# The last V unit dealt to the DMA engines in three parts, W2's remainder in two, and four casts into two result rows

## The chip, the cores and the metric

The kernel runs on one core of a Trainium2 chip. The metric is the device time of one execution in microseconds (us); lower is better. TensorE is PE in the profile (its weight loads are PEld), VectorE is DVE, ScalarE is ACT, GpSimd is POOL, and SyncE, which issues nearly all transfers, is SP. All transfers are carried out by 16 DMA engines.

## The reference

Two tokens pass through one attention block that decodes against a cache, and through one feed-forward block; a gate mixes the results. All tensors are bf16.

```python
B, Sq, D = 2, 1, 512
Hq, Hkv, Sk, Dh = 32, 32, 4096, 128      # k_cache and v_cache: (2, 32, 4096, 128), 64 MB each
Dff = 1376

g = sigmoid((x * gate_w).sum(-1, keepdims=True))
q = (x @ wq)                                             # per head
p = softmax(q @ k_cache^T * Dh ** -0.5)
a = (p @ v_cache).reshape(B, Sq, Hq * Dh) @ wo           # wo: (4096, 512)
b = relu(x @ w1) @ w2                                    # w1: (512, 1376), w2: (1376, 512)
out = g * a + (1 - g) * b                                # (2, 1, 512)
```

## The kernel before

**The caches.** K and V are each read in 16 units of 16384 rows. A unit is a `[128, 16384]` bf16 tile of `kv`: each of 128 partitions gets 128 consecutive cache rows, 32 KB in one piece. `kv` has three slots (`NSLOT`). The list `order` says in which order units are loaded: four K units, then K and V units in turn, then the last four V units (12 to 15). `place` is a unit's number in that list; slot and semaphore follow from it. SP issues unit n as soon as unit n-3 has been used up (`freed`). A transfer adds 16 to its slot's semaphore when it has landed, and `slot_wait` says which value a reader waits for.

**The work on a unit.** A K unit is transposed in four turns by DVE (`k_turn`, L381) and multiplied with the queries on PE (`k_scores`, L397) into a bank of PSUM; after every four units `sm_max`, `sm_exp` and `sm_spread` make the softmax numerators, which POOL copies to `ptm`. A V unit is multiplied on PE with them in 32 matmuls (`v_unit`, L443) and then added up from four masked pieces on DVE (`v_extract`, L454 and L457). After eight V units `o_gather` (L473 to L484) divides by the denominators, applies the gate and turns the result of one token into `oW`: 128 partitions, 32 row groups, one column for each token. The order of the work is written out by hand in one loop over 64 K turns, and a loop over V units 12 to 15 after it.

**The ends.** The result is `oW` times wo plus `hT` (the gated ReLU of x @ w1, `ffn_relu`) times w2. It is added up in one PSUM bank at column `FIN_C0`: `fin_row` (L489) multiplies one row group with four blocks of 128 columns, and block c goes to a partition group of its own, at partitions 32c onwards. `project` runs 32 row groups of wo (128 matmuls of 128 columns), `ffn_f` the 11 row groups of w2 (44 matmuls; row group 10, which has 96 rows, first). `oW` and `hT` are 32 columns wide: token 0 is column 0, token 1 is column 16, the rest is zeros from memsets on POOL (L242, L243), and `fin_row` takes 17 columns as lhsT. So the two tokens of block c come out at partitions 32c and 32c+16, with zeros between. A memset on DVE (L494) clears the bank before, one DVE cast (L508) brings all 128 partitions to `out_sb`, and the store (L276) takes every 16th partition of it, eight pieces of 256 B.

**SP's queue after the last unit.** The wo tile lies where wq and w1 were (`wreg`). In order: the last V unit (L266), eleven transfers of w2's last 96 rows (`W2A`, L271; rows 0-13, 14-26 and so on, 1 KB a row), wo in two halves (`wo0`, `wo1`, L272 and L273, 16 KB a partition each), w2's other rows in three parts (`w2b`, `w2c`, `w2d`, L275: 4, 4 and 2 KB a partition), the store. `project` waits for `wo0` at row group 0 and for `wo1` at row group 16; `ffn_f` for `w2a` at group 10, and for the other parts at groups 0, 4 and 8.

Of the kernel before, what the change touches and what calls it, by code (L numbers as in the profile page):

```python
# [3 lines left out]
dt = mybir.dt  # L4
ALU = mybir.AluOpType
ACT = mybir.ActivationFunctionType
# [6 lines left out]

NSLOT = 3
NKT = 3
W2A = ((0, 14), (14, 27), (27, 39), (39, 50), (50, 60), (60, 69), (69, 77), (77, 84), (84, 90), (90, 94), (94, 96))


class _Marker:
# [67 lines left out]
def bass_gated_mix__gqa_block_cached__dense_activation_relu__decode_kernel(  # L87
# [18 lines left out]
    sb = nc.alloc_sbuf_tensor  # L106
# [11 lines left out]
    kv = sb("kv", [128, NSLOT, 16384], dt.bfloat16)  # L118
    xTw = sb("xTw", [128, 4, 32], dt.bfloat16)
    qrow = sb("qrow", [128, 2, 4, 128], dt.bfloat16)  # L120
    wreg = sb("wreg", [128, 16384], dt.bfloat16)
    w2 = sb("w2", [128, 11, 512], dt.bfloat16)
# [18 lines left out]
    s4 = sb("s4", [32, 4, 128], dt.bfloat16)  # L141
    X2 = sb("X2", [128, 2, 8, 128], dt.float32)
    O_sb = sb("O_sb", [32, 2, 128], dt.bfloat16)
    oW = sb("oW", [128, 32, 32], dt.bfloat16)
    hT = sb("hT", [128, 11, 32], dt.bfloat16)
    out_sb = sb("out_sb", [128, 128], dt.bfloat16)

    PSF = nc.alloc_psum_tensor("PS", [128, 4096], dt.float32)
    PSB = PSF[:, :].bitcast(dt.bfloat16)
# [3 lines left out]
    def psf(p0, p1, c0, n):  # L153
        return PSF[p0:p1, c0:c0 + n]
# [8 lines left out]
    H_C0 = MISC + 72  # L163
    L_C0 = MISC + 96
    O_C0 = MISC + 128
    R_C0 = MISC + 256
    FIN_C0 = 0
# [4 lines left out]
    sem = {n: nc.alloc_semaphore("sem_" + n) for n in names}  # L172
    sem_slot = [nc.alloc_semaphore(f"sem_slot{s}") for s in range(NSLOT)]
# [3 lines left out]
    def marker(name):  # L177
        m = mk.get(name)
        if m is None:
            m = _Marker()  # L180
            mk[name] = m
        return m


    order = [("k", u) for u in range(4)]
# [3 lines left out]
    place = {what: n for n, what in enumerate(order)}  # L189

    def slot_of(what):
        return place[what] % NSLOT

    def slot_wait(what):
        return (sem_slot[slot_of(what)], 16 * (place[what] // NSLOT + 1))

    def freed(what):
        kind, u = what
# [3 lines left out]
    def pool(fn, waits=(), signal=None):  # L202
        P.add("pool", fn, waits=[marker(w) for w in waits], signal=marker(signal) if signal else None)

    def dve(fn, waits=(), signal=None, dwaits=()):
        P.add("dve", fn, waits=[marker(w) for w in waits], signal=marker(signal) if signal else None, dwaits=dwaits)

    def act(fn, waits=(), signal=None, dwaits=()):
        P.add("act", fn, waits=[marker(w) for w in waits], signal=marker(signal) if signal else None, dwaits=dwaits)

    def pe(fn, waits=(), signal=None, dwaits=()):
        P.add("pe", fn, waits=[marker(w) for w in waits], signal=marker(signal) if signal else None, dwaits=dwaits)
# [5 lines left out]
         waits=["c_i16z"], signal="c_i16")  # L218
# [8 lines left out]
         waits=["c_m3z"], signal="c_m3")  # L227
# [4 lines left out]
         waits=["c_s1"], signal="c_s2")  # L232
# [6 lines left out]
         waits=["c_s4z"], signal="c_s4")  # L239
    pool(lambda g: g.memset(selx[:], 0.0), signal="c_selx")  # L240
    pool(lambda g: g.memset(ptm[:], 0.0), signal="c_ptm")
    pool(lambda g: g.memset(hT[:], 0.0), signal="c_hT")  # L242
    pool(lambda g: g.memset(oW[:], 0.0), signal="c_oW")  # L243


    wq_in = A_wq.rearrange("(p t) n -> p (t n)", t=4)
# [6 lines left out]
    def unit_in(what):  # L253
        kind, u = what
        rows = k_rows if kind == "k" else v_rows
        return rows[u * 16384:(u + 1) * 16384, :].rearrange("(p r) d -> p (r d)", p=128)

    def sp(fn, waits=(), dwaits=()):
        P.add("sp", fn, waits=waits, dwaits=dwaits)
# [3 lines left out]
    sp(lambda e: e.dma_start(wreg[:, :], wq_in).then_inc(sem["wq"], 16))  # L263
    for n, what in enumerate(order):
        waits = [freed(order[n - NSLOT])] if n >= NSLOT else []
        sp(lambda e, what=what: e.dma_start(kv[:, slot_of(what), :], unit_in(what)).then_inc(sem_slot[slot_of(what)], 16),  # L266
           waits=waits)
        if n == 2:
            sp(lambda e: e.dma_start(wreg[:, 0:5504], w1_in).then_inc(sem["w1"], 16), waits=[marker("pe_q")])
    for p0, p1 in W2A:  # L270
# [2 lines left out]
    sp(lambda e: e.dma_start(wreg[:, 8192:16384], wo_in[:, 8192:16384]).then_inc(sem["wo1"], 16))  # L273
    for name, r0, r1 in (("w2b", 0, 4), ("w2c", 4, 8), ("w2d", 8, 10)):
        sp(lambda e, name=name, r0=r0, r1=r1: e.dma_start(w2[:, r0:r1, :], w2a_in[:, r0:r1, :]).then_inc(sem[name], 16))  # L275
    sp(lambda e: e.dma_start(out.rearrange("b s (c n) -> c (b s) n", n=128),  # L276
                             out_sb[0::16, :]).then_inc(sem["out"], 16),
       waits=[marker("dve_out")])
    sp(lambda e: e.wait_ge(sem["out"], 16))


# [83 lines left out]

    def ffn_relu():
        for b in range(2):
            dve(lambda v, b=b: v.tensor_scalar(out=hT[:, 0:10, 16 * b], in0=PSF[:, H_C0 + b:H_C0 + 20:2], scalar1=0.0,
                                               scalar2=gm[:, b:b + 1], op0=ALU.max, op1=ALU.mult),
                waits=["pe_h", "dve_gm", "c_hT"])  # L370
            dve(lambda v, b=b: v.tensor_scalar(out=hT[0:96, 10, 16 * b:16 * b + 1], in0=psf(0, 96, H_C0 + 20 + b, 1), scalar1=0.0,
                                               scalar2=gm[0:96, b:b + 1], op0=ALU.max, op1=ALU.mult),
                waits=["pe_h", "dve_gm"], signal=f"dve_h{b}")

# [47 lines left out]
    def sm_spread(g):  # L422
        dve(lambda v: v.transpose(out=ET_sb[:, :], in_=E_sb[:, :]),  # L423
            waits=[f"act_exp{g}"] + ([f"pool_pt{g - 1}_3"] if g else []), signal=f"dve_et{g}")
        for hq in range(4):
            pool(lambda e, g=g, hq=hq: e.tensor_copy(  # L426
                out=ptm[32 * hq:32 * hq + 32, g % 2, :, :, :, hq, :],
                in_=ET_sb[32 * hq:32 * hq + 32, :].rearrange("p (r u a c) -> p r u a c", r=16, u=4, a=2)),
                waits=[f"dve_et{g}", "c_oW"] + ([f"pe_v_{4 * g - 5}"] if g >= 2 else []), signal=f"pool_pt{g}_{hq}")


    def v_unit(v):
# [38 lines left out]
    def o_gather(b):  # L471
        for u in range(8):
            pe(lambda e, u=u, b=b: e.matmul(psf(0, 32, O_C0, 128), lhsT=selx[:, 28 - 4 * u:60 - 4 * u], rhs=X2[:, b, u, :],  # L473
                                            start=(u == 0), stop=(u == 7)),
               waits=[f"dve_x{8 * b + u}_3"] + ([f"dve_rinv{b}", "dve_selx"] if u == 0 else []),
               signal=(f"pe_O{b}" if u == 7 else None))
        dve(lambda v, b=b: v.tensor_scalar(out=O_sb[:, b, :], in0=psf(0, 32, O_C0, 128), scalar1=rinv[:, b:b + 1],
                                           scalar2=gb[0:32, b:b + 1], op0=ALU.mult, op1=ALU.mult),
            waits=[f"pe_O{b}", f"dve_rinv{b}", "dve_g"], signal=f"dve_O{b}")
        for dq in range(4):  # L480
            pe(lambda e, dq=dq, b=b: e.matmul(psf(0, 128, R_C0 + 32 * b, 32), lhsT=s4[:, dq, :], rhs=O_sb[:, b, 32 * dq:32 * dq + 32],
                                              start=(dq == 0), stop=(dq == 3), tile_position=(0, 0)),
               waits=([f"dve_O{b}", "c_s4"] if dq == 0 else []), signal=(f"pe_R{b}" if dq == 3 else None))
        dve(lambda v, b=b: v.tensor_copy(out=oW[:, :, 16 * b], in_=psf(0, 128, R_C0 + 32 * b, 32)), waits=[f"pe_R{b}", "c_oW"], signal=f"dve_oW{b}")  # L484


    def fin_row(r, first, last, lhsT, rhs, dw, waits, signal):
        for c in range(4):
            pe(lambda e, c=c: e.matmul(psf(32 * c, 32 * c + 17, FIN_C0, 128), lhsT=lhsT, rhs=rhs[:, c * 128:(c + 1) * 128],  # L489
                                       start=first, stop=last, tile_position=(0, 32 * c), skip_group_check=True),  # L490
               dwaits=(dw if c == 0 else []), waits=(waits if c == 0 else []), signal=(signal if c == 3 else None))

    def project():
        dve(lambda v: v.memset(psf(0, 128, FIN_C0, 128), 0.0), waits=["act_exp2"], signal="dve_fin0")  # L494
        for r in range(32):
            dw = {0: [(sem["wo0"], 16)], 16: [(sem["wo1"], 16)]}.get(r, [])
            fin_row(r, r == 0, False, oW[:, r, 0:17], wreg[:, r * 512:(r + 1) * 512], dw,
                    ["dve_oW0", "dve_oW1", "act_exp3", "dve_fin0"] if r == 0 else [], None)

    def ffn_f():  # L500
        for n, r in enumerate([10, *range(10)]):
            m = 96 if r == 10 else 128
            dw = {10: [(sem["w2a"], 16 * len(W2A))], 0: [(sem["w2b"], 16)], 4: [(sem["w2c"], 16)], 8: [(sem["w2d"], 16)]}.get(r, [])
            fin_row(r, False, r == 9, hT[0:m, r, 0:17], w2[0:m, r, :], dw, ["dve_h0", "dve_h1"] if n == 0 else [],
                    "pe_fin" if r == 9 else None)

    def store():
        dve(lambda v: v.tensor_copy(out=out_sb[:, :], in_=psf(0, 128, FIN_C0, 128)), waits=["pe_fin"], signal="dve_out")  # L508


    gate()
# [74 lines left out]
```

## Time and profile before

| | us |
|---|---|
| median of three runs (lowest, highest) | 347.75 (347.29, 347.83) |
| the profiled execution | 347.82 |
| its span, first to last instruction | 346.6 |
| PE busy, DVE busy | 201.8, 183.6 |
| ACT busy, POOL busy | 13.9, 22.1 |
| DMA: bytes read, mean rate over the span | 145.43 MB, 420 GB/s |
| mean granted TensorE clock | 0.818 |

The profile is of one execution. Its busy times and its timeline are counted from the start of the span; the execution's own time is 1.2 us longer than the span. Beside each engine's instructions the trace has every DMA packet with its start, duration and size, though not which DMA engine moved it. In an answer on waits, a line gives who waited, for whom, and then the time in total, how often, and the longest; in the timeline, a line gives start, duration, engine, line of the kernel, operation, output and input, and in brackets the idle time before it with what ended it.

### The profile page before, as it was taken

What the parts mean: (1) busy time and instruction counts of PE and PEld (TensorE: products, weight loads), DVE (VectorE), ACT (ScalarE), POOL (GpSimd) and SP (SyncE); (2) the same over time, 40 slices, a digit from 0 to 9 for tenths busy, and PEclk for the clock granted to TensorE, in tenths of its full rate; (3) what the DMA queues carried; (4) which work ended last, traced back from release to release, by engine and by line L of the source; (5) the groups of instructions that cost most, each with busy time, mean ns of one, the idle gap of its engine ahead of it and who ended that gap; (6) DMA issues with size and microseconds to landing.
All of it is one profiled execution on the core that took longest, in us unless ns stands there. A gap on an engine that the chain in (4) does not pass through costs nothing.

```text
span 346.6 us, 3023 instructions
## 1 busy us (share of the span) xinstructions
PE 201.8 (58%) x1318; PEld 77.5 (22%) x1334; DVE 183.6 (53%) x177; ACT 13.9 (4%) x48; POOL 22.1 (6%) x38
## 2 busy tenths in 40 slices
PE   0339969773845739174845739174885639422283
PEld 0213344221211213021211213021421213110052
DVE  0858777991908355391908365391648267211120
ACT  1040000000000000000000000000000000000000
POOL 8500000020000000020000000020000000200000
PEclk9999978999685958789695969589698969666578
DMA  8999999999999999999999999999999999999993
GB/s 314 446 446 427 402 447 435 444 427 424 424 425 428 442 439 431 429 427 427 427 433 435 439 431 425 427 431 427 435 441 431 427 431 427 419 435 442 393 409 151
DMA packets 5838, 145.61 MB, mean 420 GB/s; under 512 B 735, under 2 KB 834, under 8 KB 1218
## 3 DMA queue, kind: packets, MB, share of 16 engines
q1 hardware_dynamic: 5820, 145.43, 98.1%
q8 instruction: 10, 0.16, 0.2%
q14 instruction: 2, 0.02, 0.0%
q10 hardware_dynamic: 6, 0.00, 0.0%
HBM read 145.43 MB, written 0.00 MB: 420 GB/s over the span
## 4 chain that ended last, share of the span: by engine, by line
DMA 71%; DVE 16%; PE 10%; SPq 2%; issue 1%; DVEq 0%
DMA kv<-in_A_k_cache_dram 53%; DVE kt L381 12%; DMA w<-in_B_w_dram 10%; DMA kv<-in_A_v_cache_dram 8%; PE PS L397 6%; PE PS L443 4%; DVE X L457 1%; SPq L271 1%; DVE mpad L407 1%; DVE ET L423 1%; PE PS L489 0%; DVE X L454 0%; SPq L266 0%; DVE mrow L409 0%; DVE mmax L410 0%
## 5 line engine op out<-in xcount | busy, mean ns | idle before, releaser
L397 PE MATMUL PS<-kt,qbuf 128*128 128x512 bf16 x496 | 146.6, 447 | 95.1 <-DVE kt L381 92.2
L381 DVE STREAM_TRANSPOSE kt<-kv 128x2048 f32<-128x2048 f32 x64 | 144.0, 2285 | 101.5 <-DMA kv<-in_A_k_cache_dram 98.8
L397 PEld LDWEIGHTS PS<-kt,qbuf 128*128 128x128 bf16 x512 | 50.6, 108 | 189.1 <-DVE kt L381 116.5
L443 PE MATMUL PS<-kv,ptm 128*16 128x512 bf16 x512 | 37.2, 442 | 23.0 <-DMA kv<-in_A_v_cache_dram 23.0
L426 POOL COPY ptm<-ET 32x512 bf16<-32x512 bf16 x16 | 9.7, 607 | 275.1 <-DVE ET L423 274.4
L443 PEld LDWEIGHTS PS<-kv,ptm 128*16 128x16 bf16 x512 | 12.8, 98 | 45.8 <-issue 35.8
L454 DVE TENSOR_SCALAR X<-PS,maskc 128x128 f32<-128x128 f32 x16 | 5.1, 319 | 30.9 <-PE PS L443 30.9
L457 DVE SCALAR_TENSOR_TENSOR X<-PS,maskc,X 128x128 f32<-128x128 f32 x48 | 16.8, 351 | 1.7
L352 ACT ACTIVATE qbuf<-PS 32x4 bf16<-32x4 bf16 x32 | 5.7, 178 | 109.2 <-PE PS L397 108.6
L418 ACT ACTIVATE E<-PS,negm 128x512 bf16<-128x512 f32 x4 | 2.7, 687 | 154.5 <-DVE negm L414 154.5
L473 PE MATMUL PS<-X,selx 128*32 128x128 f32 x32 | 5.5, 346 | 0.0
L289 DVE COPY xTw<-xT 128x8 bf16<-128x8 bf16 x1 | 5.1, 5054 | 0.0
L489 PE MATMUL PS<-wreg,oW 128*17 128x128 bf16 x128 | 2.8, 257 | 3.8 <-DMA wreg<-in_A_wo_dram 3.2
L473 PEld LDWEIGHTS PS<-X,selx 128*32 128x32 f32 x32 | 4.6, 147 | 1.9 <-issue 1.4
L284 PE MATMUL PS<-ident,x_sb 3*128 3x3 bf16 x4 | 0.3, 166 | 8.2 <-POOL s L236 8.2
L290 DVE TENSOR_TENSOR xg<-xT 128x8 f32<-128x8 bf16 x1 | 4.9, 4858 | 0.0
L362 PE MATMUL PS<-xT,wreg 128*128 128x2 bf16 (+1 forms) x44 | 2.8, 200 | 3.2 <-DMA wreg<-in_B_w_dram 3.2
L287 DVE COPY xT<-PS 128x12 bf16<-128x12 bf16 x1 | 0.2, 170 | 8.5 <-PE PS L284 8.5
L508 DVE CAST out_sb<-PS 128x128 bf16<-128x128 f32 x1 | 0.3, 291 | 7.9 <-PE PS L489 7.9
L220 POOL MEMSET qbuf<- 128x5120 bf16 x1 | 4.4, 4370 | 0.0
L294 PE MATMUL PS<-xgs,ones 128*128 128x2 f32 x2 | 0.6, 364 | 5.6 <-DVE xgs L292 5.6
L407 DVE TENSOR_REDUCE mpad<-PS 128x1 f32<-128x512 f32 x4 | 2.7, 676 | 2.1 <-PE PS L397 2.1
(60 smaller groups left out, 45.2 us busy)
## 6 DMA issues: line engine op xcount, KB each, us to landing
kv<-in_A_k_cache_dram SPq DMA_DIRECT2D x16, 4096.0 KB, 26.2
kv<-in_A_v_cache_dram SPq DMA_DIRECT2D x16, 4096.0 KB, 18.7
wreg<-in_A_wq_dram SPq DMA_DIRECT2D x1, 4096.0 KB, 12.3
wreg<-in_A_wo_dram SPq DMA_DIRECT2D x2, 2048.0 KB, 30.4
wreg<-in_B_w_dram SPq DMA_DIRECT2D x1, 1376.0 KB, 25.4
w<-in_B_w_dram SPq DMA_DIRECT2D x2, 512.0 KB, 33.8
w<-in_B_w_dram SPq DMA_DIRECT2D x1, 256.0 KB, 34.4
x_sb<-in_A_x_dram ACTq DMA_DIRECT2D x1, 2.0 KB
```

Source lines behind the costliest of these rows:

```text
L220: pool(lambda g: g.memset(qbuf[:], 0.0), signal="c_qbuf")
L289: dve(lambda v: v.tensor_copy(out=xTw[:, :, 0:2], in_=xT), waits=["dve_xT", "c_xTw"], signal="dve_xTw")
L290: dve(lambda v: v.tensor_tensor(out=xg[:], in0=xT, in1=xT3[:, :, 2:3].to_broadcast([128, 4, 2]), op=ALU.mult), waits=["dve_xT"], signal="d ...
L352: act(lambda a, out=out, src=src: a.activation(out=out, in_=src, func=ACT.Copy), waits=[f"pe_sc_{4 * uh + 3}"], signal=f"q_1_{uh}_{hq}")
L381: dve(lambda v: v.transpose(out=dst, in_=pairs[:, :, 32 * k:32 * k + 32, :]), waits=([f"pe_sc_{i - NKT}"] if i >= NKT else []), dwaits=([s ...
L397: pe(lambda e, j=j, pos=pos, c=c, cc=cc: e.matmul(psf(0, 128, (g % 2) * BANK, 512), lhsT=qbuf[:, u % 8, j, 32 - pos:160 - pos], rhs=kt16[: ...
L407: dve(lambda v, g=g: v.tensor_reduce(out=mpad[:, 0:1], in_=psf(0, 128, (g % 2) * BANK, 512), axis=AX.X, op=ALU.max), waits=[f"pe_sc_{16 * ...
L426: pool(lambda e, g=g, hq=hq: e.tensor_copy(out=ptm[32 * hq:32 * hq + 32, g % 2, :, :, :, hq, :], in_=ET_sb[32 * hq:32 * hq + 32, :].rearra ...
L443: pe(lambda e, n=n, t=t, a=a, r16=r16, grp=grp, u4=u4, rows=rows: e.matmul(psf(32 * t, 32 * t + 16, V_B * BANK, 512), lhsT=ptm[:, grp % 2, ...
L454: dve(lambda e, src=src, dst=dst: e.tensor_scalar(out=dst, in0=src, scalar1=maskc[:, 0:1], scalar2=None, op0=ALU.mult), waits=[f"pe_v_{v}" ...
L457: dve(lambda e, src=src, dst=dst, c=c: e.scalar_tensor_tensor(out=dst, in0=src, scalar=maskc[:, c:c + 1], in1=dst, op0=ALU.mult, op1=ALU.add),
L473: pe(lambda e, u=u, b=b: e.matmul(psf(0, 32, O_C0, 128), lhsT=selx[:, 28 - 4 * u:60 - 4 * u], rhs=X2[:, b, u, :], start=(u == 0), stop=(u ...
```

## The change

The last V unit is issued as three transfers into the same slot, under the same semaphore: partitions 0 to 111, 112 to 124 and 125 to 127 (112 rows over all DMA engines, 13 over engines 0 to 12, 3 over engines 0 to 2). `slot_wait` counts the three. W2's last 96 rows are issued as 91 and 5 rows, no longer in eleven pieces. `oW` and `hT` are two columns wide, their memsets and that of the PSUM bank are gone, and a matmul of `fin_row` writes two partitions. Four casts, two on DVE and then two on ACT, bring the four blocks to two rows of `out_sb`, and the store writes two rows of 1 KB.

```diff
-W2A = ((0, 14), (14, 27), (27, 39), (39, 50), (50, 60), (60, 69), (69, 77), (77, 84), (84, 90), (90, 94), (94, 96))
+W2A = ((0, 91), (91, 96))
+DEAL = ((0, 112), (112, 125), (125, 128))
...
-    oW = sb("oW", [128, 32, 32], dt.bfloat16)
-    hT = sb("hT", [128, 11, 32], dt.bfloat16)
-    out_sb = sb("out_sb", [128, 128], dt.bfloat16)
+    oW = sb("oW", [128, 32, 2], dt.bfloat16)
+    hT = sb("hT", [128, 11, 2], dt.bfloat16)
+    out_sb = sb("out_sb", [2, 512], dt.bfloat16)
...
+    def pieces(what):
+        return DEAL if what == order[-1] else ((0, 128),)
+
     def slot_wait(what):
-        return (sem_slot[slot_of(what)], 16 * (place[what] // NSLOT + 1))
+        return (sem_slot[slot_of(what)], 16 * (place[what] // NSLOT + len(pieces(what))))
...
-    pool(lambda g: g.memset(hT[:], 0.0), signal="c_hT")
-    pool(lambda g: g.memset(oW[:], 0.0), signal="c_oW")
...
-        sp(lambda e, what=what: e.dma_start(kv[:, slot_of(what), :], unit_in(what)).then_inc(sem_slot[slot_of(what)], 16),
-           waits=waits)
+        for p0, p1 in pieces(what):
+            sp(lambda e, what=what, p0=p0, p1=p1: e.dma_start(kv[p0:p1, slot_of(what), :], unit_in(what)[p0:p1, :])
+               .then_inc(sem_slot[slot_of(what)], 16), waits=(waits if p0 == 0 else []))
...
-    sp(lambda e: e.dma_start(out.rearrange("b s (c n) -> c (b s) n", n=128),
-                             out_sb[0::16, :]).then_inc(sem["out"], 16),
-       waits=[marker("dve_out")])
+    sp(lambda e: e.dma_start(out.rearrange("b s n -> (b s) n"), out_sb[:, :]).then_inc(sem["out"], 16),
+       waits=[marker("dve_out"), marker("act_out")])
...
-            pe(lambda e, c=c: e.matmul(psf(32 * c, 32 * c + 17, FIN_C0, 128), lhsT=lhsT, rhs=rhs[:, c * 128:(c + 1) * 128],
+            pe(lambda e, c=c: e.matmul(psf(32 * c, 32 * c + 2, FIN_C0, 128), lhsT=lhsT, rhs=rhs[:, c * 128:(c + 1) * 128],
...
-        dve(lambda v: v.memset(psf(0, 128, FIN_C0, 128), 0.0), waits=["act_exp2"], signal="dve_fin0")
...
-        dve(lambda v: v.tensor_copy(out=out_sb[:, :], in_=psf(0, 128, FIN_C0, 128)), waits=["pe_fin"], signal="dve_out")
+        def piece(c):
+            return out_sb[:, 128 * c:128 * c + 128], psf(32 * c, 32 * c + 2, FIN_C0, 128)
+
+        for c in range(2):
+            dst, src = piece(c)
+            dve(lambda v, dst=dst, src=src: v.tensor_copy(out=dst, in_=src), waits=["pe_fin"], signal=("dve_out" if c else None))
+        for c in range(2, 4):
+            dst, src = piece(c)
+            act(lambda a, dst=dst, src=src: a.activation(out=dst, in_=src, func=ACT.Copy), waits=["pe_fin"],
+                signal=("act_out" if c == 3 else None))
```

## The prediction

> **What bounds the kernel now.** First the page's slices:
>
> ```profile
> DMA  8999999999999999999999999999999999999993
> ```
>
> The 16 DMA engines are busy from the first slice to the last but one, while no compute engine is. So the end is set by the bytes, and by how evenly the engines finish. Next the busy time by stage, in the windows of the tail (columns: window, length, busy time and instructions of PE, PEld, DVE, ACT, POOL, the granted clock, the DMA share, GB/s):
>
> ```profile
> 325.00:329.20 4.20, 0.04 (x4) 0.07 (x8) 0.00 (x0) 0.00 (x0) 0.00 (x0) 0.50 1.01 371
> 336.60:341.00 4.40, 1.12 (x68) 0.94 (x72) 0.00 (x0) 0.00 (x0) 0.00 (x0) 1.00 0.89 363
> 341.00:344.50 3.50, 3.23 (x108) 2.40 (x108) 0.00 (x0) 0.00 (x0) 0.00 (x0) 0.52 0.15 57
> ```
>
> Until 336 us DMA is full; from 341 us a few late engines carry 57 GB/s. The waits of the tail say who waits for them:
>
> ```profile
> PE PS L443 <- DMA kv<-in_A_v_cache_dram: 6.4, 1, 6.4
> PE PS L489 <- DMA wreg<-in_A_wo_dram: 3.2, 1, 3.2
> PE PS L489 <- DMA w<-in_B_w_dram: 0.2, 1, 0.2
> ```
>
> PE waits for the last V unit, for the second half of wo and for the w2 parts, each a transfer that every engine has a share of. The timeline shows the end word for word:
>
> ```profile
> 329.16 3.59 PE L443 MATMUL PS<-kv,ptm 128*16 128x512 bf16 x32 [6.37 <-DMA kv<-in_A_v_cache_dram]
> 336.43 0.17 DVE L494 MEMSET PS<- 128x128 f32 x1
> 336.65 1.07 PE L489 MATMUL PS<-wreg,oW 128*17 128x128 bf16 x64 [0.58 <-DVE PS L494]
> 340.95 1.75 PE L489 MATMUL PS<-wreg,oW 128*17 128x128 bf16 x64 [3.23 <-DMA wreg<-in_A_wo_dram]
> 343.43 1.03 PE L489 MATMUL PS<-w,hT 128*17 128x128 bf16 x24 [0.20 <-DMA w<-in_B_w_dram]
> 344.52 0.29 DVE L508 CAST out_sb<-PS 128x128 bf16<-128x128 f32 x1 [7.92 <-PE PS L489]
> 344.84 0.65 SPq L276 DMA_DIRECT2D out_dram<-out_sb  x1
> ```
>
> Last, the trace's DMA packets (start, duration, bytes; no engine's name). A packet starts 3 to 4 ns before the one ahead of it on its engine ends, so they can be chained into 16 rows of packets. Each has 264 of 32 KB; the numbers of 1 KB packets are 11, 11, 10, 10, 9, 9, 8, 7, 6, 5, 4, 3, 2, 1, 0, 0, as eleven W2A pieces of n rows on engines 0 to n-1 give. I number the chains by that (two with the same count can't be told apart). Four things are read there:
> - A 32 KB packet has a mean of 1.218 us on every chain, so no engine is slower than another.
> - What sets engines apart is single stops: a 16 KB packet of the instruction queue sits about 1.0 us on one engine, which loses about 1.5 us by it. Nine fall between 41.7 and 333.7 us, the last on engine 6.
> - Engines without a stop end the last V unit at 326.5 to 327.2 us, those with one at 328.3 to 328.9.
> - Behind the V unit, a chain's time to the end of wo's first half, less eight 16 KB packets (8 x 0.608 = 4.87), is 1.0 to 1.45 us on engines 0 to 7, 0.58 on 8, 0.35 on 9 and 0.1 to 0.3 on 10 to 15. So many tiny packets cost more than their own 46 ns each: the three wo packets after them are slowed by about 0.3 us each.
>
> Engine 6 ends last, at 343.9 us, then 2 or 3 (342.8) and 5 (342.4); the rest between 339.9 and 342.0.
>
> **The change, part by part.** The profiled run took 347.82 us (span 346.6 and 1.2 around it); the median is 347.75. I count from 347.82.
>
> *W2A in two transfers.* Engines 0 to 12 get seven 1 KB rows under one completion, 0 to 4 one more with another. That is 8 to 10 packets instead of engine 6's 16; the nearest row is engine 9 (10 packets, 0.35 us). Engine 6 loses 1.10 us now by the same working, stop taken out, so it gains 0.75 us, and wo's second half, w2b, w2c and w2d come that much earlier together. Bounds: nothing (the excess is not the number of packets) and 1.0.
>
> *SP's queue.* Five issues stand for the last unit and W2A where twelve did; W2A's eleven took 4.0 us (the chain's SPq L271), 0.36 each, so SP is done some 2.5 us earlier. At 303 us, when they are issued, the engines still have two units ahead of them, so nothing comes of it. The new slot count asks for all three parts; the unit's V matmuls still start at the last landing. Only the first of the three waits for the buffer.
>
> *The rows dealt 112, 13, 3.* Engines 0 to 2 move nine rows, 3 to 12 eight, 13 to 15 seven. By packets alone engine 2 gains a row (1.22) and loses 0.93 of W2A's excess: 342.82 + 0.29 = 343.1 us, level with engine 6 at 343.9 - 0.75 = 343.15. The lightened 13 to 15 (339.9 to 342.0) weren't last, so nothing is won there.
>
> What the trace doesn't show is a large transfer narrower than 128 partitions. In every large one, eight rows per engine follow each other at 1.218 us (26.9 GB/s), and whether the engine sets this, or the entry into the partitions that it serves, can't be read. Here thirteen neighbouring partitions are written at once by 13 engines, then three more. Lower bound: the engine sets it, 1.22 us for a row, nothing extra. Upper bound: the entry does, eight partitions to one as eight rows go to one engine; then partitions 112 to 127 have two entries, 8 x 1.22 = 9.74 us where 1.22 was counted, 8.5 extra. The 112 rows, seven a piece, then no longer match engines and entries one to one: up to one row, 1.2, more. No end is near: the only narrow transfers, W2A's, aren't free (up to 1.45 us for 96 KB), which speaks against the lower one, and sixteen partitions with only two entries would need the worst layout. I take the middle by ratio: the square root of 8 rows on one entry, 2.83 x 1.218 = 3.44 us, so 2.2 extra, and half of 1.2 for the 112 rows: 2.8 together.
>
> The Trainium skill has a rule here (SBUF — State Buffer, Door 1: The DMA port swizzle): partitions reach memory by 16 ports of about 27 GB/s, and 112 to 127 lie on four of them, so that few neighbours are slow however many engines write. By it, as an estimate from that page, sixteen rows take four rows' time, 4.9 us, 3.65 extra, and the whole sum would be about 352 us. No run here shows it.
>
> Is it hidden? Not by compute: wo and w2 stand behind these rows on the same engines, so each late row moves the end. The V path has more room: the unit would land near 332.7 (engine 2: 328.65 + 1.22 + 2.8), wo's first 64 matmuls would start 7.3 us later as now, at 340.0, and end at 341.1, before wo's second half at 340.95 + 2.0.
>
> *Memsets.* L494's 0.17 us goes, and up to 0.2 us of wait at 336.65; wo's second half is 3.2 us away, so nothing. hT's and oW's on POOL (0.38 and 0.94 us at 12.4 us) delayed nobody. lhsT of 2 columns instead of 17: the matmuls still move 128 columns each at a granted clock of 0.52; between 0 and 0.1, I take nothing.
>
> *Casts and store.* Two casts on DVE for one: a cast of 128x32 took 0.297 us and of 128x128 0.291, so the length isn't what they cost; two in a row are 0.6, that is 0.31 more. ACT's two start with them; 178 ns at 4 columns and 687 at 512 put 128 columns at 0.30, so they end together. The store's issue was 0.65 us with eight pieces; W2A's two-row issue took 0.25, so up to 0.40 less. Together -0.09 (bounds -0.3 and +0.4).
>
> Sum: -0.75 + 2.8 - 0.09 = +1.96, so 349.8 us.
>
> **The rivals.**
> 1. *Each engine keeps its pace* (other side). No extra for narrow rows: 347.82 - 0.75 - 0.09 = 347.0, faster. For it: all 16 chains run at one pace whatever else goes on. It decides if the narrow rows cost below 0.15 us.
> 2. *The gains fall out and the rows cost nothing*: W2A's excess stays on engines 2 and 6, engine 2 gets a ninth row (342.82 + 1.22 = 344.04, 0.14 later than now), the two casts cost 0.31 and the issue stays: 348.3, no change that counts. For it: the slowed wo packets all lie on engines 0 to 8, which may be a matter of which engines and not of how many packets.
> 3. *Entries of eight partitions*: 347.82 + 8.5 + 1.2 - 0.84 = 356.7, by the upper bound.
>
> Against 1 and 2 speaks that the trace has no large transfer but those in which engines and partitions match one to one.
>
> **How the numbers follow.** Forecast 0.48, rival 3 0.18, rival 1 0.17, rival 2 0.17. About 0.2% (0.7 us) is what a measurement of this kernel can tell from no change. Faster is rival 1 (0.17), same rival 2 (0.17), slower the forecast and rival 3 (0.66). The range goes from rival 1 (346.9) to short of rival 3's end (355.5); the forecast's own is 348.6 to 354, its extra between 1.6 and 7.
>
> **What would show it.** Right: the V unit lands after 330 us with the 32 KB packets of its last two parts well over 1.22 us; DMA's last slices fall off more slowly; PE's wait for wo (L489) grows beyond 3.2; the first wo packets on low engines are no longer slowed. Wrong: all 32 KB packets stay at 1.22 us and the last w2 packet ends before 343.9 us (rival 1); an engine 0 to 2 is last by one row (rival 2). The store step is right if the SP issue is about 0.25 us and the casts end 0.6 us after the last matmul.

## The result, and the profile after

The changed kernel took 362.07 us (median of 4 runs) against 347.52 for the kernel before: ratio 1.0416, 95% interval 1.0402 to 1.0431 (so in all brackets below), 14.5 us more. The forecast was slower, but 349.8 us, and the range ended at 355.5.

The slices of the changed kernel (share of busy time of the DMA engines in tenths, and what they moved), with the second row of the kernel before ahead of them:

```profile
GB/s 314 446 446 427 402 447 435 444 427 424 424 425 428 442 439 431 429 427 427 427 433 435 439 431 425 427 431 427 435 441 431 427 431 427 419 435 442 393 409 151
```

```profile
DMA  8999999999999999999999999999999999999995
GB/s 347 412 449 427 439 416 441 429 412 460 412 440 428 419 456 410 441 430 423 447 416 438 434 423 443 419 434 438 421 441 423 434 432 424 441 277 226 110 363 231
```

The row of shares is as before: the engines have packets in hand nearly to the end. What they moved isn't. From the 36th slice on, three slices run at 277, 226 and 110 GB/s. The DMA engines are busy, and move little. So a row of nines says only that packets are under way. The windows of the last stage put times to it (before, and then after, columns as in the prediction; a packet counts whole in the window in which it starts, so a share can pass 1):

```profile
315.00:327.00 12.00, 3.59 (x32) 1.06 (x32) 1.40 (x4) 0.00 (x0) 0.00 (x0) 0.59 1.01 426
```

```profile
315.00:327.00 12.00, 3.59 (x32) 1.06 (x32) 1.40 (x4) 0.00 (x0) 0.00 (x0) 0.52 1.04 262
327.00:333.00 6.00, 0.00 (x0) 0.00 (x0) 0.00 (x0) 0.00 (x0) 0.00 (x0) 0.50 1.21 232
333.00:344.00 11.00, 0.00 (x0) 0.00 (x1) 0.00 (x0) 0.00 (x0) 0.00 (x0) 0.50 0.84 119
344.00:354.00 10.00, 7.73 (x120) 4.63 (x123) 2.00 (x6) 0.00 (x0) 0.00 (x0) 0.72 0.98 412
```

Before, 426 GB/s; after, 262 and 232 while the 112 rows run, 119 with the 13 and the 3, and 412 as soon as whole transfers of 128 partitions (wo) follow. In the packet records the 32 KB packets take mostly 2.0 to 2.5 us while the 112 rows run and 3.3 to 5.1 us from 332 us on, where they took 1.22.

The waits of PE in the tail, after:

```profile
PE PS L445 <- DMA kv<-in_A_v_cache_dram: 19.3, 1, 19.3
PE PS L491 <- DMA wreg<-in_A_wo_dram: 1.5, 1, 1.5
```

The wait for the last V unit went from 6.4 to 19.3 us, that for wo's second half from 3.2 to 1.5. The timeline of the end, after:

```profile
344.03 3.59 PE L445 MATMUL PS<-kv,ptm 128*16 128x512 bf16 x32 [19.29 <-DMA kv<-in_A_v_cache_dram]
351.45 1.06 PE L491 MATMUL PS<-wreg,oW 128*2 128x128 bf16 x64 [0.29 <-DVE oW L486]
353.98 1.06 PE L491 MATMUL PS<-wreg,oW 128*2 128x128 bf16 x64 [1.46 <-DMA wreg<-in_A_wo_dram]
357.54 0.55 ACT L517 ACTIVATE out_sb<-PS 2x128 bf16<-2x128 f32 x2 [62.32 <-PE PS L491]
357.54 0.57 DVE L514 CAST out_sb<-PS 2x128 bf16<-2x128 f32 x2 [6.14 <-PE PS L491]
358.18 0.27 SPq L279 DMA_DIRECT2D out_dram<-out_sb  x1
```

The V matmuls start at 344.03 instead of 329.16, 14.9 us late, and wo's second half comes at 353.98 instead of 340.95, 13.0 us late. The end follows.

### The profile page after: what moved, and what is told of

It reads as the page before. It is cut to its first block, busy times and chain, and to the rows that moved or that the text cites. A ratio compares the mean times of both kernels' runs of the same rounds, so it can differ in the third digit from the quotient of the medians.

```text
span 359.4 us, 3032 instructions
## 1 busy us (share of the span) xinstructions
PE 203.5 (57%) x1334; PEld 76.6 (21%) x1334; DVE 182.7 (51%) x177; ACT 14.4 (4%) x50; POOL 20.9 (6%) x36
## 4 chain that ended last, share of the span: by engine, by line
DMA 72%; DVE 14%; PE 11%; SPq 1%; issue 1%; DVEq 0%
DMA kv<-in_A_k_cache_dram 51%; DMA w<-in_B_w_dram 14%; DVE kt L383 11%; DMA kv<-in_A_v_cache_dram 7%; PE PS L399 7%; PE PS L445 4%; DVE X L459 1%; DVE mpad L409 1%; SPq L269 0%; PE PS L491 0%; DVE X L456 0%; DVE mrow L411 0%; SPq L274 0%; DVE mmax L412 0%; DVE ET L425 0%
## 5 line engine op out<-in xcount | busy, mean ns | idle before, releaser
L399 PE MATMUL PS<-kt,qbuf 128*128 128x512 bf16 x512 | 150.8, 449 | 93.6 <-DVE kt L383 93.4
L291 DVE COPY xTw<-xT 128x8 bf16<-128x8 bf16 x1 | 4.1, 4087 | 0.0
L323 PE MATMUL PS<-wreg,xTw 128*32 128x512 bf16 x32 | 3.6, 628 | 0.0
L292 DVE TENSOR_TENSOR xg<-xT 128x8 f32<-128x8 bf16 x1 | 3.6, 3631 | 0.0
L364 PEld LDWEIGHTS PS<-xT,wreg 128*128 128x128 bf16 (+1 forms) x44 | 2.7, 160 | 3.9 <-DMA wreg<-in_B_w_dram 3.9
## 6 DMA issues: line engine op xcount, KB each, us to landing
wreg<-in_A_wq_dram SPq DMA_DIRECT2D x1, 4096.0 KB, 12.3
```

Of the source, the lines that this page charges most:

```text
L291: dve(lambda v: v.tensor_copy(out=xTw[:, :, 0:2], in_=xT), waits=["dve_xT", "c_xTw"], signal="dve_xTw")
L364: return e.matmul(psf(0, m, H_C0 + 2 * ft, 2), lhsT=cols, rhs=xT3[:, t, 0:2], start=(t == 0), stop=(t == 3))
L399: pe(lambda e, j=j, pos=pos, c=c, cc=cc: e.matmul(psf(0, 128, (g % 2) * BANK, 512), lhsT=qbuf[:, u % 8, j, 32 - pos:160 - pos], rhs=kt16[: ...
```

## The experiments

Theory E: the pace of a transfer is set by the entry into the partitions that it writes at one time. The rivals were that rows lying side by side in memory slow each other on the reading side, that several transfers in flight do it, that any unit other than one transfer of 128 rows is slow, that the uneven deal itself costs the time, and that W2A or the casts have part of it.

**Every shape by itself.**

```diff
+    for n, (to, rows) in enumerate(SHAPES):     # slices of partitions, slices of rows
+        e.dma_start(kv[to, :], unit(n)[rows, :]).then_inc(sems[n], 16)
+        e.wait_ge(sems[n], 16)
```

> The kernel computes nothing (its output is zeros): SP issues sixteen loads of 32 KB rows one after another, each only when the one before has landed, so that every shape is timed alone. In the changed kernel's trace the 32 KB packets take about 2.0 to 2.5 us while the 112-row part runs and 4.0 to 5.0 us in the 13- and 3-row parts, against 1.22 in full units. Theory E (the entry into the partitions sets the pace; neighbouring partitions share one): duration goes with the partitions written, not with the rows read. 128 rows: 1.2 us a packet; 13, 3 and 16 rows at partitions 112 and up: 3.6 to 4.9; the same sixteen partitions filled from every 8th row: 3.6 to 4.9 too; sixteen partitions 8 apart: 1.2 to 2.4, also when their rows are neighbours in memory; 32 neighbours: about 2.4, 32 partitions 4 apart: less than that; 64 neighbours 2.4; 4 neighbours 4.9; 112 alone above 1.5. Rival R (reading side: rows that lie side by side in memory slow each other): duration goes with the rows read; partitions 112 to 127 from every 8th row then take 1.2 us, partitions 8 apart from neighbouring rows 4 and more. Rival C (company: the slowdown comes from three transfers in flight at once and two engine positions out of step, not from a shape): every shape alone takes 1.2 to 1.3 us a packet.

From the packet records, first packet's start to last one's end:

| partitions written | rows read | total us | median packet us |
|---|---|---|---|
| 0-127 (first and last time) | 0-127 | 10.9, 10.8 | 1.21 |
| 0-111 | 0-111 | 15.1 | 2.03 |
| 112-124 | 112-124 | 4.3 | 3.78 |
| 125-127 | 125-127 | 3.1 | 2.94 |
| 112-127 | 112-127 | 4.4 | 3.83 |
| 112-127 | every 8th | 4.5 | 3.74 |
| every 8th | every 8th | 3.2 | 2.24 |
| every 8th | 112-127 | 2.4 | 2.10 |
| 0-31 | 0-31 | 5.4 | 2.55 |
| every 4th (32) | every 4th | 3.5 | 1.35 |
| 0-63 | 0-63 | 10.8 | 2.56 |
| every 2nd (64) | every 2nd | 6.1 | 1.21 |
| 0-95 | 0-95 | 15.1 | 2.37 |
| 0-119 | 0-119 | 20.5 | 2.54 |
| 0-3 | 0-3 | 3.6 | 3.29 |

The windows of that run show it too, for 112 neighbours, 64 neighbours, 64 partitions 2 apart, and 128 (window, length, DVE, POOL, clock, DMA share, GB/s):

```profile
14.00:29.00 15.00, 0.00 (x0) 0.00 (x0) 1.00 0.89 234
77.80:88.60 10.80, 0.00 (x0) 0.00 (x0) 1.00 0.91 194
90.50:96.60 6.10, 0.00 (x0) 0.00 (x0) 1.00 0.87 333
142.80:153.70 10.90, 0.00 (x0) 0.00 (x0) 1.00 0.95 385
```

64 rows take 10.8 us as neighbours and 6.1 two apart: 194 or 333 GB/s at nearly the same DMA share. There the rows read change along with the partitions; sixteen rows were tried crosswise. With the partitions kept and the rows read changed (112-127 from every 8th row) next to nothing moves, 4.4 and 4.5 us; with the rows kept and the partitions spread, 4.4 us become 2.4. With partitions 8 apart, neighbouring rows were the faster ones (2.4 us against 3.2), the opposite of rival R. So the reading side is out for sixteen rows; for the larger shapes the cross wasn't tried. Company with other transfers is out, since each shape ran alone. And 112 rows took 15.1 us where 128 took 10.9: fewer rows, more time.

Two expectations were missed: 3 and 4 neighbours took 2.9 and 3.3 us a packet, where 3.6 or more and 4.9 were expected. Each shape but the first ran once.

**Undoing the deal alone, and doing it alone.**

```diff
-DEAL = ((0, 112), (112, 125), (125, 128))
+DEAL = ((0, 128),)
```

> The changed kernel with the last V unit in one transfer of 128 rows again; W2A in two transfers and the four casts stay. Theory E (the narrow parts cost everything): the whole loss goes, the V unit's matmuls start near 329 us again, and what is left are the prediction's other two terms, -0.75 and -0.09: ratio to before 0.995 to 1.000 (346.0 to 347.6 us). Rival W (part of the loss is W2A's 91 rows over 13 engines or the casts): the ratio stays above 1.005.

347.32 us against 347.28: ratio 1.0002 (0.9993 to 1.0011). The loss is gone. The two other terms' gain of 0.84 us didn't come: the ratio is just above what they allowed.

The other way round, the kernel before with `DEAL` and `pieces` put in and nothing else:

```diff
+DEAL = ((0, 112), (112, 125), (125, 128))
...
+        for p0, p1 in pieces(what):
...
```

> The kernel before with the last V unit in three transfers of 112, 13 and 3 rows, nothing else changed. Theory E: nearly the whole loss, ratio 1.040 to 1.047, the V unit's matmuls start near 344 us. Rival W: clearly less than the changed kernel's loss, below 1.035.

362.94 us, ratio 1.0450 (1.0434 to 1.0466). The V unit's matmuls, first without and then with the deal:

```profile
329.59 3.59 PE L445 MATMUL PS<-kv,ptm 128*16 128x512 bf16 x32 [6.61 <-DMA kv<-in_A_v_cache_dram]
```

```profile
345.30 3.59 PE L448 MATMUL PS<-kv,ptm 128*16 128x512 bf16 x32 [19.88 <-DMA kv<-in_A_v_cache_dram]
```

Together: the deal by itself makes the whole loss, and W2A and the casts add nothing to it. The deal alone even lost about 1.1 us more than the whole change (15.7 against 14.5), so beside the deal the other parts may save something. The two were measured in different sessions, and no run settles where that microsecond comes from.

**The casts alone.** The kernel with one transfer of 128 rows and with eleven W2A pieces:

```diff
-DEAL = ((0, 112), (112, 125), (125, 128))
+DEAL = ((0, 128),)
-W2A = ((0, 91), (91, 96))
+W2A = ((0, 14), (14, 27), (27, 39), (39, 50), (50, 60), (60, 69), (69, 77), (77, 84), (84, 90), (90, 94), (94, 96))
```

> The kernel before with the casts part alone (columns 2 wide, no memsets, four casts, store of two rows); W2A in eleven pieces and the V unit in one transfer. By the prediction's term: -0.09 us (bounds -0.3 and +0.4), ratio 0.999 to 1.001; in the profile the casts take 0.28 us more and the store's issue 0.38 us less than before.

347.24 us, ratio 1.0001 (0.9993 to 1.0010): no difference that can be told. Its profile has the two steps as expected:

```profile
344.10 0.57 DVE L514 CAST out_sb<-PS 2x128 bf16<-2x128 f32 x2 [7.76 <-PE PS L491]
344.74 0.27 SPq L279 DMA_DIRECT2D out_dram<-out_sb  x1
```

0.57 us for 0.29 and 0.27 for 0.65.

**Two halves, near or spread.** Two transfers of 64 rows each, four packets an engine, in both kernels; they differ in which partitions, and so which rows, go together.

```diff
-DEAL = ((0, 112), (112, 125), (125, 128))
+DEAL = ((0, 128, 2), (1, 128, 2))          # even, then odd (first, end, step)
+DEAL = ((0, 64, 1), (64, 128, 1))          # in the other kernel: low, then high
```

> The changed kernel with the last V unit in two transfers of 64 rows, the even partitions and then the odd ones. Theory E (the partitions written at one time set the pace): 64 partitions 2 apart ran at 1.21 us a packet when alone, so nothing is lost: ratio to before 0.998 to 1.003, the V unit's matmuls start at 329 to 330 us. Rival N (any unit that isn't one transfer of 128 rows is slow, by its shape or by being several transfers): as slow as the low and high halves, ratio above 1.02.

> The changed kernel with the last V unit in two transfers of 64 rows, partitions 0 to 63 and then 64 to 127: rows a transfer, rows an engine and number of transfers as with even and odd partitions. Theory E: 64 neighbours ran at 2.5 us a packet when alone, so eight packets an engine take 10 us more than at 1.22, less what engines that are in different halves at one time give back (up to a third): ratio 1.018 to 1.032, the V unit's matmuls start at 335 to 340 us. Rival N: the same ratio as even and odd partitions, whatever it is.

Even and odd: 347.30 us, ratio 0.9999 (0.9990 to 1.0008). Low and high: 359.58 us, 1.0352 (1.0335 to 1.0369). The same window of both, even and odd first:

```profile
327.00:333.00 6.00, 3.80 (x35) 1.58 (x36) 0.17 (x1) 0.00 (x0) 0.00 (x0) 0.50 0.99 404
```

```profile
327.00:333.00 6.00, 0.00 (x0) 0.00 (x0) 0.24 (x1) 0.00 (x0) 0.00 (x0) 0.66 0.99 208
```

The DMA share is 0.99 in both, the bytes are half, and PE has nothing to do in the second. Rival N is out: two transfers cost nothing in one kernel and 12 us in the other. With the cross of sixteen rows, in which the rows read made no difference, this shows E in the kernel itself. The loss of 12.3 us and the start of the V unit's matmuls (341.75 us) were a little above the ranges expected, and above the 10 us reckoned with nothing given back.

**The 112 rows alone.**

```diff
-DEAL = ((0, 112), (112, 125), (125, 128))
+DEAL = ((0, 112),)
```

> The changed kernel without the 13- and the 3-row transfers: partitions 112 to 127 of the last V unit aren't loaded, so its time is that of the 112-row part alone. Seven packets an engine. By the changed kernel's packets (2.0 to 2.5 us while this part runs) it costs 7 x 1.1 = 7.7 us, less the one row that each engine no longer moves (1.2): ratio 1.015 to 1.022. If the prediction's bound had held (one row, 1.2 us, at most), it would be at 0.996 to 1.001, and the two narrow transfers would be the whole loss.

355.60 us, ratio 1.0240 (1.0225 to 1.0255): 8.3 us more than before, with one row an engine fewer, and a little above the range expected. So the two narrow transfers account for the rest, 362.07 - 355.60 = 6.5 us (6.1 by the ratios, since the two runs are of different sessions), and the wide one for the larger part.

**An uneven deal without neighbours.** Two tries:

```diff
-DEAL = ((0, 112), (112, 125), (125, 128))
+DEAL = ((0, 128, 2), (1, 128, 4), (3, 107, 4), (107, 128, 4))
```

> The changed kernel with its rows dealt unevenly, but by partitions spread over all 128: 64 rows 2 apart, 32 rows 4 apart, 26 rows 4 apart (13 engines, two each), 6 rows 4 apart (6 engines). Engines 0 to 5 move nine rows, 6 to 12 eight, 13 to 15 six. Theory E: an uneven deal costs nothing by itself; at most the 26 rows run at 2.4 instead of 1.2 us (2.4 us in all): ratio 0.998 to 1.008. Rival D (the uneven deal itself, nine rows on engines that stood at eight, is a good part of the loss): above 1.01.

352.42 us, ratio 1.0151 (1.0136 to 1.0166): outside what E gave, in the range of rival D. The packet records have the 26-row and the 6-row transfers' packets mostly at 2.1 to 2.8 us, one at 3.1, the ones before at 1.22. Two rows at 2.3 cost 2.2 us, and the ninth row of engines 0 to 5, which I had left out of that expectation, 2.3 to 3 more: about 5, which is what was lost. But that is arithmetic, so D was tried by itself, with nine and seven rows an engine in transfers of eight partitions 4 apart:

```diff
+DEAL = ((0, 128, 2, 0, 16384), (1, 128, 4, 0, 16384), (3, 128, 4, 0, 8192),      # last two: columns
+        (3, 32, 4, 8192, 16384), (35, 64, 4, 8192, 16384), (67, 96, 4, 8192, 16384), (99, 128, 4, 8192, 16384))
```

> The changed kernel with an uneven deal of the same size (two rows between the heaviest and the lightest engine) that never writes to neighbours: 64 rows 2 apart, 32 rows 4 apart, half of the columns of the last 32 rows, and their other half in four transfers of eight rows 4 apart, which engines 0 to 7 alone carry. Engines 0 to 7 move nine rows, 8 to 15 seven. Theory E: one row more on engines 0 to 7 and at most as much again where they meet engines 8 to 15 at the same partitions: 1.2 to 2.4 us, ratio 1.002 to 1.007. Rival D (the uneven deal itself costs as much as the strided deal lost, 5 us): ratio 1.012 to 1.018.

350.18 us, ratio 1.0085 (1.0071 to 1.0099): 2.9 us, above E's 1.2 to 2.4 and below D's 4 to 6. Its 32 KB packets all stay at 1.22; the 16 KB packets between 326 and 332 us take 0.9 to 1.2 us on the mean instead of 0.61, while the four narrow transfers run beside wo's. So this uneven deal cost about 1.7 us more than its extra row. Whether the unevenness does that, or narrow transfers beside wide ones, the run can't separate; no uneven deal gained.

**The same deal in the middle.**

```diff
-        return DEAL if what == order[-1] else ((0, 128),)
+        return DEAL if what == order[16] else ((0, 128),)
...
+        more = 2 if slot_of(what) == 16 % NSLOT and place[what] >= 16 else 0
+        return (sem_slot[slot_of(what)], 16 * (place[what] // NSLOT + 1 + more))
```

> The changed kernel with the three transfers (112, 13 and 3 rows) on a K unit in the middle, the seventeenth in the order, and the last V unit in one transfer. Theory E: the lost time is DMA time, and DMA has no slack anywhere, so the loss is the same as at the end, ratio 1.035 to 1.046. Rival T (it costs so much because it is the tail, where nothing follows that could fill in and every wait is seen): in the middle the engines that are done early go on with the next units, and clearly less is lost, ratio below 1.025.

359.10 us, ratio 1.0339 (1.0325 to 1.0354): 11.8 us of the 14.5, a little under E's range and far above T's. The tail isn't what makes it dear; some 2.7 us fewer are lost where units follow.

## Why the prediction was wrong

**The narrow rows, +2.8 us taken, about +14.5 measured.** The sign was right, and the mechanism was one of the two that the prediction put its value between: the entry into the partitions, and not the engine, sets the pace. The sizes failed, in two terms:
- *The 112 rows.* "Up to one row, 1.2, more" was the bound and half of it the value. Measured: 8.3 us more than before although each engine moves one row (1.2 us) less, so 9.5 us for the term. This is the step that put the result outside the range: with 9.5 in place of 0.6 the sum is 358.7 us, past 355.5, while the other term alone would have stayed inside. The bound counted how many rows an entry must take in all. The runs show a pace in its place: alone, 112 neighbours took 15.1 us (243 GB/s) and 128 took 10.9 (385 GB/s). That engines meet at one entry at each of their seven steps, while other entries stand idle, is the likely reason, but it is argued and not shown.
- *The last sixteen rows.* 2.2 us extra taken between 0 and 8.5. Measured: 6.1 to 6.5 us, of which 1.2 is the row that engines 0 to 12 move anyhow, so about 5. The bounds held; the middle by ratio was too low. Alone, sixteen neighbours took 4.4 us, and the 13 rows and the 3 rows took 4.3 and 3.1.

The Trainium skill's rule (SBUF — State Buffer, Door 1: The DMA port swizzle: 16 ports, and 112 to 127 on four of them) gave 4.9 us for sixteen rows as an estimate; alone they took 4.4. With the prediction's other terms that estimate makes 351.2 us, not the 352 written there. The page's measured rates for 32 and 64 neighbours, 189 and 196 GB/s, agree with the run of shapes: 32 rows of 32,768 bytes in 5.44 us are 193 GB/s, 64 in 10.75 are 195. By the rule four neighbours share one port of about 27 GB/s; here they ran at 37, and the measurement decides. I weighed the rule for the last sixteen rows only. The same page's remark that 64 partitions are no faster than 32 says that the number of partitions doesn't decide, which was a reason to doubt the bound for the 112 rows; a time for them it doesn't give.

What stays open is which partitions each engine takes in such a transfer. Blocks of neighbours (seven to an engine for 112, eight for 120), with two engines at an entry at each step, would fit 120 rows at 2.5 us a packet and 64 neighbours at 2.6; 64 partitions 2 apart at 1.21 would not fit them. Packets carry no engine and no partition, so no run here settles it.

**W2A, -0.75 us taken, nothing measured.** Without the deal, two W2A transfers gave 347.32 us and eleven 347.24, with casts in both. The working was right as far as it went: from the kernel before to the one with two W2A transfers and no deal, the excess over 0.612 us of the 16 KB packets that start before 331.5 us, added over all engines, fell from 7.4 to 5.5 us in the profiles. The step that failed is that this excess on engine 6 sets the end. The term was taken from engine 6 because it was last, and by the chained packets it was last because two instruction packets had stopped it, at 41 and 333 us. In another build that engine is another one. The engine that ended last carried eight W2A pieces in the kernel before (343.5 us) and one piece in the kernel with the casts alone (343.2 us); with two W2A transfers and no deal the end was 343.1 us, again on an engine with two stops. What an engine carries in W2A hardly matters beside two stops of about 1.6 us each. This is read from single profiles and wasn't tried by itself.

**Casts and store, -0.09 us.** +0.28 and -0.38 in the profile, where +0.31 and -0.40 were worked out; the ratio of the kernel with the casts alone can't tell it from nothing. **Memsets**, nothing: they are gone in the same kernel, and no difference shows.

**Hidden or not.** The V path stayed hidden, but by less than said: wo's second half still came last, with a wait of 1.5 us where I foresaw one that grows beyond 3.2. The V unit was late by 14.9 us and wo's second half by only 13.0, so the wait shrank; that sign was wrong. The first sign named, 32 KB packets well over 1.22 us and a V unit after 330, was right.

**The rivals.** "Each engine keeps its pace" is out. "The gains fall out and the rows cost nothing" came true in its first half only. "Entries of eight partitions" gave 356.7, nearer than the forecast, but its 1.2 us for the 112 rows was the same mistake.

One correction: the packet times in the prediction were counted from a wrong zero and are 0.36 us late (engine 6 ended at 343.54 us, not 343.9). Differences between them, which the sum used, aren't touched.

## What to carry to other kernels

Where a load has to be split, try partitions that lie apart over the whole range before neighbours: two transfers of 64 rows cost nothing as even and odd partitions here and 12 us as low and high ones. Read DMA's GB/s beside its busy share, since 0.99 can be 404 or 208 GB/s. And before moving a row between DMA engines to even out their ends, ask what made the late one late: here, by the profiles, stops by single packets, on another engine in another build.

## What was not expected of the hardware

112 neighbouring partitions took longer (15.1 us) than 128 (10.9), and 120 longer still (20.5), on 15 engines with eight rows each (15 completion packets stand behind the 120 rows, 16 behind the others). A 16 KB instruction packet takes about 1.0 us on one DMA engine: engines with one such stop ended the last V unit at about 328.1 us in the profile before, those without at 326.5. Nine came by 334 us, and in the three profiles whose packets were chained the engine that ended last was one with two of them. Four neighbours were filled at 37 GB/s (131,072 bytes in 3.56 us), above one engine's 26.9.
